# An attention and expert kernel: the first expert's weight splits, its row gather and the loop's tail put in another order

## The chip, the cores and the metric

One core of a Trainium2 chip runs the whole program in one launch. The metric is the device time of the execution in microseconds (us), the median of several runs.

## The reference

Two steps follow each other. Attention: 8 batches, 8 heads, 576 positions, 64 channels; heads 0 to 3 look at a local band of 32 positions, heads 4 to 7 at every 32nd position:

```python
scores = np.where(masks, q @ k.transpose / sqrt(D), -1e9)
x = softmax(scores) @ v                # then 4608 tokens of 512 channels
```

Then a mixture of 8 experts with one expert a token. A token with `x @ w_skip <= 0` is passed through; any other goes to the expert with the largest logit:

```python
e = argmax(x @ w_gate);  gate = softmax(x @ w_gate)[e]
out = x + gate * (relu(x @ w1[e]) @ w2[e])   # w1: 512 x 1024, w2: 1024 x 512
```

## The kernel before, in words

**The attention loop.** The main loop runs over 32 iterations (b, pr): 8 batches and in each four units of blocks, pr 0 and 1 of the local heads, pr 2 and 3 of the strided ones. An iteration issues the score products of the unit two ahead (`qk`, L200), the value products of the unit before (`pv`, L273 and L287), transposes and exponentials of its own (`tex`, L243 on PE, L251 on ACT) and the transposes of the finished output of two units before (`xpose`, L331 and L341). DVE adds the mask (`sm`, L207 to L214), finds the maxima (`mx`, L220) and scales the output (`x`, L300); POOL subtracts the maxima (L223).

**Routing.** When a group of batches is through, `score` multiplies its tokens with the gate (L387), `route1` transposes the scores (L406) and finds expert and gate on DVE (`rm`, L414, and the steps behind it), with the gate sums on POOL (L434 to L438). `route2` ranks the tokens (L447 to L454) and gives each its slot (`rdi`, L463); `scat` then writes tile after tile into a table in DRAM, by indirect transfers of POOL (L476).

**The first expert.** After batch 3 the expert with the most tokens so far is picked. For it, 288 of its tokens of batches 0 to 5 are taken early: `rows` reads their table rows (`tab`, L621), `gather` fetches the tokens from DRAM (`xg`, three indirect transfers of 96 rows, L633), and `xturn` transposes them on PE (L655). Its weights come in eight pieces of 512 KB, j 0 to 3 of w1 and 4 to 7 of w2: `wdma` fetches one into one of three buffers `raw` (L581, SP), `wcast` casts it on ACT (`w1h`, L593), and `wrest` takes the rest on DVE (`w1l`, L598). The products then take three matmuls for one: high by high, high by low, low by high. While the loop runs, all four pieces of w1 and the first of w2 are fetched, and the four are split.

**Behind the loop.** `ffn1a` computes the first two groups of hidden channels (L700, L704, with `hout` at L673 and L674), then `ffn1` the other six, with the last batch's routing in between; then come the second product and seven more experts.

**What sets the order.** Within the loop POOL, PE, DVE and SP keep the order in which the code is written (a manual schedule, L847); ACT is not among them there, its order is laid out by the scheduler. Behind the loop PE, ACT and DVE are in written order. Each engine works its own queue in order and waits at an instruction whose input isn't there.

Of the kernel before, what the change touches and what calls it, by code (L numbers as in the profile page):

```python
# [39 lines left out]
COUNTED = {4: 3, 7: 5}  # L40
PB = 3
CB = 5
SPLITS = [(6, 0), (6, 1), (7, 0), (7, 2)]
FETCH = [(6, 0), (6, 1), (6, 3), (7, 0)]
CE = (96, 3)
WHOLE = range(6)

# [52 lines left out]
def attn_moe(ctx: ExitStack, tc: tile.TileContext, q, k, vl, vh, vs, w9d, w1d, w2d, cst, out, NB=B):  # L100
    nc = tc.nc
    V, A, G, T = nc.vector, nc.scalar, nc.gpsimd, nc.tensor
# [413 lines left out]
    def count(b):  # L516
        n, _ = cnt_[b]
        t2 = constp.tile([1, NE], F32, name="pt2")
        V.tensor_tensor(t2, first, n, op=ALU.mult)
        r2 = constp.tile([1, 1], F32, name="pr2")  # L520
        V.tensor_reduce(r2, t2, axis=AX.X, op=ALU.add)
        V.scalar_tensor_tensor(fsel[:, 2:3], r2, float(CE[0] * CE[1]), fsel[:, 1:2], op0=ALU.min, op1=ALU.add)
        V.tensor_copy(isel[:, 2:3], fsel[:, 2:3])
# [64 lines left out]
    def wcast(key, j):  # L588
        raw = raw_.pop((key, j))
        pl, tg, nb = (early, "w1", 4) if j < 4 else (pool["h"], "w2", 2) if j < 6 else (pool["b"], "w2", 4)  # L590
        hi = pl.tile([128, 1024], F32R, name=tg + "h", tag=tg + "h", bufs=nb)
        lo = pl.tile([128, 1024], F32R, name=tg + "l", tag=tg + "l", bufs=nb)
        A.copy(hi, raw)  # L593
        cast_[key, j] = raw, hi, lo

    def wrest(key, j):
        raw, hi, lo = cast_.pop((key, j))
        V.tensor_tensor(lo, raw, hi.bitcast(F32), op=ALU.subtract)  # L598
        wt[key, j] = (hi, lo)

    def wsplit(key, j0, j1):
        for j in range(j0, j1):
            wcast(key, j)
            wrest(key, j)
# [214 lines left out]
    def run(*gs):  # L819
        weave(gs, [])  # L820
# [32 lines left out]
    for n, (b, pr) in enumerate(units):  # L853

        if n == 4:
            tv = table.rearrange("(p a n) c -> p a (n c)", p=128, a=5)
            fills = [(tv[:, a], fill.rearrange("p n c -> p (n c)")) for a in range(5)]
        if pr % 2 == 0:
            vj = jobs_v(b + 1, pr // 2) if b + 1 < NB else []
            g = n // 2 + 3  # L860
            qk_ = jobs_qk(g // 2, g % 2) if g // 2 < NB else [None] * 4
            ob = jobs_out(units[n - 4][0], units[n - 4][1] // 2) if n > 3 else [[], []]
            steps = [vj[0:1], vj[1:], ob[0], qk_[0:1], qk_[1:2], qk_[2:3], qk_[3:4], ob[1]]
            steps = [[x for x in y if x is not None] for y in steps]
        if n + LA >= len(units) and "h" not in pool:
            zctx.close()
            pool["h"] = ctx.enter_context(tc.tile_pool(name="hpool", bufs=1, side="right", reuse_waits="tile"))
        g = [i for i, x in enumerate(GROUPS) if x[1] == b]

        front = [qk(*units[n + LA])] if n + LA < len(units) else []  # L870
        if n > 0:
            front.append(pv(*units[n - 1]))
        seq = [tex(b, pr)]
        if g and pr == 2:
            seq = [xpose(*units[n - 2])] + seq
        for x in front[:-1]:
            next(x)
        hand()

        if len(front) > 1:  # L880
            run(seq.pop(0))
        hand()
        next(front[-1])
        hand()
        issue(fills[0:1], mark[0].ins)
        del fills[0:1]
        rank = []
        if ranked is not None:
            rank = [route2(ranked, of=COUNTED.get(b - 1))]
            for _ in range(tiles(ranked) + 1):  # L890
                next(rank[0])
            ranked = None

        if b > CB:
            run(*late)
            late = []
        for x in front:
            next(x, 0)
        run(*rank, *late, *front)
        late = []  # L900
        if cast_:
            wrest(*list(cast_)[0])
        if b > 0 and pr == 2:
            seq = [score(b - 1)] + [rest_out(b - 1)] * (b - 1 in WHOLE) + seq
        if n > 1 and not (g and pr == 2):
            seq.append(xpose(*units[n - 2]))
        run(*seq)
        hand()
        if pr == 3:
            issue(rest_, mark[0].ins)  # L910
            del rest_[:]
        if g and pr == 2:
            late = [route1(g[0])]
            next(late[0])
        if g and pr == 3:
            if b > CB:
                run(route2(g[0], of=COUNTED.get(b)))
            else:
                ranked = g[0]
        if b == PB + 2 and pr == 2:  # L920
            pick(PB)
        if (b, pr) in SPLITS:
            j = SPLITS.index((b, pr))
            wcast("e", j)
        if b == CB + 2 and pr == 3:
            count(CB)
        if n == 0 or pr == 3 and b + 1 < NB:
            for m in range(2):
                shift(b + (n > 0), m)
        if n == 1:  # L930
            for g in range(len(GROUPS)):
                payload(g)
        for _ in range(3 if b > CB else 2):
            if sc_ and n + 1 < len(units):
                scat(*sc_.pop(0))
        if b == PB + 2 and pr == 3:
            e0 = nc.sync.value_load(isel[0:1, 0:1], min_val=0, max_val=NE - 1)
            wdma("e", e0, 0, 1)
        if b == PB + 2 and pr == 3:
            s0 = G.value_load(isel[0:1, 1:2], min_val=0, max_val=(NE - 1) * ESTR)  # L940
        if (b, pr) in FETCH:
            j = FETCH.index((b, pr)) + 1
            wdma("e", e0, j, j + 1)
        if b == CB + 2:
            if pr == 0:
                assert not sc_
            if pr == 1:
                rows("e", s0, *CE, eng=G)
                gather("e", "e", "e", last=(CB + 1) * S)
    pool_order.close()  # L950
    nr = len(GROUPS) - 1
    while sc_:
        scat(*sc_.pop(0))
    with tc.manual_schedule(engines={T.engine, A.engine, V.engine}):
        run(pv(*units[-1]), xpose(*units[-2]), xturn("e"), xpose(*units[-1]))
    for kind in range(2):
        for part in jobs_out(NB - 1, kind):
            issue(part)
# [3 lines left out]
    psum, bufs = pctx.enter_context(tc.tile_pool(name="psumT", bufs=1, space=PSUM, reuse_waits="tile")), {"S": 2, "T": 3, "PV": 2, "R": 1}  # L962
    ga = ffn1a("e")
    with tc.manual_schedule(engines={T.engine, A.engine, V.engine}):
        run(ga, score(NB - 1))
        g = ffn1("e", 2, 6)
        run(islice(g, 4), later(route1, nr), islice(g, 4), later(route2, nr))
        while sc_:
            scat(*sc_.pop(0))
        wsplit("e", 4, 5)  # L970
        places = sort(NB - 1)
        run(g)
        rest = places()
        actx.close()
        pool["b"] = ctx.enter_context(tc.tile_pool(name="bpool", bufs=1, reuse_waits="tile"))
        wsplit("e", 5, 6)
        run(ffn1("e", 6, 8))
# [155 lines left out]
```

## Time and profile before

| | us |
|---|---|
| runs: median (lowest to highest of 3) | 447.95 (439.43 to 449.22) |
| the profiled execution, its own time | 444.14 |
| its span, first to last instruction | 442.4 |
| PE busy | 410.5 (93%) |
| DVE, ACT, POOL busy | 256.6, 197.7, 163.0 |

The attention loop ends near 167 us, the experts fill the rest. A row of a timeline names its start, its duration, engine, line, output and inputs, and in brackets the idle time of the engine just before it with what ended it. A busy PE is not PE at its peak: the granted clock (PEclk) stands beside it, 1.00 for 2.4 GHz and 0.50 for 1.2 GHz.

### The profile page before, as it was taken

How to read it: one execution, taken by the hardware profiler on the slowest of the kernel's cores; microseconds unless marked ns; L12 is line 12 of the kernel's file. 1: busy time of each engine (PE TensorE's matmuls, PEld its weight loads, DVE VectorE, ACT ScalarE, POOL GpSimd, SP SyncE). 2: the span in 40 equal slices, each digit the busy share in tenths (PEclk: the TensorE clock that was granted, in tenths of full speed). 3: DMA queues.
4: the chain of work that ended last, by engine and by line, in shares of the span. 5: the costliest groups of instructions: out<-in, count | busy, mean ns of one | idle time of the engine just before them, and what ended most of it. 6: DMA issues, size and time to landing. Idle time of an engine off the chain costs nothing.

```text
span 442.4 us, 12541 instructions
## 1 busy us (share of the span) xinstructions
PE 410.5 (93%) x5111; PEld 373.4 (84%) x5112; DVE 256.6 (58%) x500; ACT 197.7 (45%) x382; POOL 163.0 (37%) x205
## 2 busy tenths in 40 slices
PE   5999998999976984999999999999999999999994
PEld 3878787787765774899898799999999999999984
DVE  3686767659854964352494654474574554855611
ACT  1566373745626543342633434353543544554400
POOL 3353427745783667254043235022024122200201
PEclk8799999999988897999999999999999999999999
DMA  8999899999998536443557377365575565645201
GB/s 278 363 315 304 266 315 264 265 293 284 218 265 273 135 81 170 110 97 90 192 176 237 102 220 241 100 203 158 180 218 177 172 211 177 216 156 163 70 21 43
DMA packets 48758, 86.47 MB, mean 195 GB/s; under 512 B 9811, under 2 KB 25939, under 8 KB 48697
## 3 DMA queue, kind: packets, MB, share of 16 engines
q1 hardware_dynamic: 41017, 75.22, 56.1%
q0 software_dynamic: 7680, 10.42, 8.4%
q8 instruction: 41, 0.67, 0.6%
q14 instruction: 20, 0.16, 0.1%
HBM read 70.58 MB, written 15.63 MB: 195 GB/s over the span
## 4 chain that ended last, share of the span: by engine, by line
PE 53%; DMA 4%; issue 2%; POOL 2%; DVE 0%; POOLq 0%; ACT 0%; ACTq 0%
PE S L661 15%; PE S L663 15%; PE S L662 15%; DMA xg<-out_dram,tab 2%; DMA table<-pay,rdi 2%; PE T L655 2%; PE PV L753 2%; POOL xg L633 1%; PE S L700 1%; PE PV L795 0%; POOL table L476 0%; DMA tab<-table 0%; PE PV L794 0%; PE PV L793 0%; PE T L387 0%
## 5 line engine op out<-in xcount | busy, mean ns | idle before, releaser
L741 POOL DMA_INDIRECT out_dram<-ot,tab x25 | 27.9, 1117 | 149.2 <-DVE ot L739 135.7
L661 PE MATMUL S<-xh,w1h 128*128 128x342 f32 (+6 forms) x248 | 78.5, 316 | 0.3 <-DVE hl L674 0.3
L663 PE MATMUL S<-xh,w1l 128*128 128x342 f32 (+6 forms) x248 | 76.7, 309 | 0.0
L662 PE MATMUL S<-xl,w1h 128*128 128x342 f32 (+6 forms) x248 | 76.6, 309 | 0.0
L661 PE MATMUL S<-hh,w2h 128*128 128x288 f32 (+5 forms) x192 | 59.3, 309 | 0.0
L663 PE MATMUL S<-hh,w2l 128*128 128x288 f32 (+5 forms) x192 | 58.1, 303 | 0.0
L662 PE MATMUL S<-hl,w2h 128*128 128x288 f32 (+5 forms) x192 | 57.9, 302 | 0.0
L673 ACT ACTIVATE hh<-S 128x342 fp32r<-128x342 f32 (+6 forms) x64 | 28.0, 437 | 65.9 <-PE S L663 58.7
L598 DVE TENSOR_TENSOR w1l<-raw,w1h 128x1024 fp32r<-128x1024 f32 x32 | 39.3, 1232 | 27.0 <-ACT w1h L593 27.0
L661 PEld LDWEIGHTS S<-xh,w1h 128*128 128x128 f32 x248 | 46.9, 189 | 1.1 <-DVE hl L674 0.6
L598 DVE TENSOR_TENSOR w2l<-raw,w2h 128x1024 fp32r<-128x1024 f32 x32 | 39.0, 1223 | 13.7 <-ACT w2h L593 9.6
L200 PE MATMUL S<-kt,qt 64*64 64x54 f32 (+1 forms) x1280 | 33.6, 248 | 14.3 <-issue 4.3
L662 PEld LDWEIGHTS S<-xl,w1h 128*128 128x128 f32 x248 | 46.8, 189 | 0.1
L663 PEld LDWEIGHTS S<-xh,w1l 128*128 128x128 f32 x248 | 46.7, 188 | 0.0
L633 POOL DMA_INDIRECT xg<-out_dram,tab x25 | 32.5, 1302 | 35.3 <-PE T L655 13.9
L674 DVE SCALAR_TENSOR_TENSOR hl<-S,hh 128x342 fp32r<-128x342 f32 (+6 forms) x64 | 31.0, 484 | 24.0 <-ACT hh L673 23.8
L200 PEld LDWEIGHTS S<-kt,qt 64*64 64x64 f32 x1280 | 27.8, 145 | 19.8 <-DVE sm L207 6.8
L476 POOL DMA_INDIRECT table<-pay,rdi x38 | 39.7, 1044 | 10.8 <-issue 7.3
L223 POOL TENSOR_TENSOR sm<-sm,mx 128x384 f32<-128x384 f32 (+1 forms) x32 | 29.2, 935 | 35.8 <-DVE mx L220 29.3
L663 PEld LDWEIGHTS S<-hh,w2l 128*128 128x128 f32 x192 | 36.2, 189 | 0.1
L662 PEld LDWEIGHTS S<-hl,w2h 128*128 128x128 f32 x192 | 36.3, 189 | 0.0
L661 PEld LDWEIGHTS S<-hh,w2h 128*128 128x128 f32 x192 | 36.2, 188 | 0.0
(168 smaller groups left out, 828.3 us busy)
## 6 DMA issues: line engine op xcount, KB each, us to landing
raw<-in_w_dram SPq DMA_DIRECT2D x64, 512.0 KB
vt<-in_vs_dram SPq DMA_DIRECT2D x16, 390.0 KB
qt<-in_qp_dram SPq DMA_DIRECT2D x16, 304.0 KB
kt<-in_kp_dram SPq DMA_DIRECT2D x16, 297.0 KB
kt<-in_kp_dram SPq DMA_DIRECT2D x14, 304.0 KB
vt<-in_vl_dram SPq DMA_DIRECT2D x16, 260.0 KB
out_dram<-x SPq DMA_DIRECT2D x16, 256.0 KB
qt<-in_qp_dram SPq DMA_DIRECT2D x14, 288.0 KB
```

Source lines behind the costliest of these rows:

```text
L200: mark[0] = T.matmul(s[HP * (i ^ j):HP * (i ^ j) + HP, j, (blk - b0) * win:(blk - b0 + 1) * win], lhsT=qt[p, j, blk * nq:blk * nq + HP], r ...
L223: G.tensor_tensor(e[:, j], sw[:, j], mx[:, j].unsqueeze(2).broadcast_to([128, b1 - b0, win]), op=ALU.subtract)
L476: i = G.indirect_dma_start(out=table, out_offset=bass.IndirectOffsetOnAxis(ap=di[:, t:t + 1], axis=0), in_=pay[:, t, :], in_offset=None, b ...
L598: V.tensor_tensor(lo, raw, hi.bitcast(F32), op=ALU.subtract)
L633: i = G.indirect_dma_start(out=xg[:s["P"], t, :], out_offset=None, in_=out[0:last, :], in_offset=bass.IndirectOffsetOnAxis(ap=s["tab"][:s[ ...
L655: T.transpose(t[:, j * P:(j + 1) * P], s["xg"][:P, j, c * 128:(c + 1) * 128], ident[:P, :P])
L661: T.matmul(p, lhsT=a[0], rhs=b[0], start=start, stop=False)
L662: T.matmul(p, lhsT=a[0], rhs=b[1], start=False, stop=False)
L663: T.matmul(p, lhsT=a[1], rhs=b[0], start=False, stop=stop)
L673: A.activation(s["hh"][:, f, :C], p[:, :C], AF.Relu)
L674: V.scalar_tensor_tensor(s["hl"][:, f, :C], p[:, :C], 0.0, s["hh"][:, f, :C].bitcast(F32), op0=ALU.max, op1=ALU.subtract)
L741: i = G.indirect_dma_start(out=out, in_=ot[:P], in_offset=None, bounds_check=NTOK - 1, oob_is_err=False, out_offset=bass.IndirectOffsetOnA ...
```

## The change

Four things change. The splits of the first expert's pieces 0, 1 and 2 go from iterations (6,0) to (7,3) into (6,3) to (7,3): casts in (6,3), (7,0), (7,1), rests in (7,1), (7,2), (7,3); piece 3 is split behind `ffn1a`. The fetches follow: pieces 0 to 2 in (6,0), (6,1), (6,3), where pieces 1 to 3 were, and pieces 3 and 4 in (7,2) and (7,3). The scatters left over in (7,0) are issued ahead of that iteration's POOL work, and the gather of the first expert's tokens goes from (7,1) to (7,3), behind the gate sums of batch 6. At the loop's end `route2` of batch 6 stands behind the last `pv`, and the last `xpose` and the last batch's `score` stand ahead of `xturn`.

```diff
@@ -40,8 +40,9 @@
 COUNTED = {4: 3, 7: 5}
 PB = 3
 CB = 5
-SPLITS = [(6, 0), (6, 1), (7, 0), (7, 2)]
-FETCH = [(6, 0), (6, 1), (6, 3), (7, 0)]
+CASTS = [(6, 3), (7, 0), (7, 1)]
+RESTS = [(7, 1), (7, 2), (7, 3)]
+FETCH = [(6, 0), (6, 1), (6, 3), (7, 2), (7, 3)]
 CE = (96, 3)
 WHOLE = range(6)
 
@@ -896,10 +897,13 @@
             late = []
         for x in front:
             next(x, 0)
+        if b == CB + 2 and pr == 0:
+            while sc_:
+                scat(*sc_.pop(0))
         run(*rank, *late, *front)
         late = []
-        if cast_:
-            wrest(*list(cast_)[0])
+        if (b, pr) in RESTS:
+            wrest("e", RESTS.index((b, pr)))
         if b > 0 and pr == 2:
             seq = [score(b - 1)] + [rest_out(b - 1)] * (b - 1 in WHOLE) + seq
         if n > 1 and not (g and pr == 2):
@@ -913,17 +917,14 @@
             late = [route1(g[0])]
             next(late[0])
         if g and pr == 3:
-            if b > CB:
+            if b == CB + 1:
                 run(route2(g[0], of=COUNTED.get(b)))
             else:
                 ranked = g[0]
         if b == PB + 2 and pr == 2:
             pick(PB)
-        if (b, pr) in SPLITS:
-            j = SPLITS.index((b, pr))
-            wcast("e", j)
-        if b == CB + 2 and pr == 3:
-            count(CB)
+        if (b, pr) in CASTS:
+            wcast("e", CASTS.index((b, pr)))
         if n == 0 or pr == 3 and b + 1 < NB:
             for m in range(2):
                 shift(b + (n > 0), m)
@@ -935,24 +936,26 @@
                 scat(*sc_.pop(0))
         if b == PB + 2 and pr == 3:
             e0 = nc.sync.value_load(isel[0:1, 0:1], min_val=0, max_val=NE - 1)
-            wdma("e", e0, 0, 1)
         if b == PB + 2 and pr == 3:
             s0 = G.value_load(isel[0:1, 1:2], min_val=0, max_val=(NE - 1) * ESTR)
         if (b, pr) in FETCH:
-            j = FETCH.index((b, pr)) + 1
+            j = FETCH.index((b, pr))
             wdma("e", e0, j, j + 1)
         if b == CB + 2:
             if pr == 0:
                 assert not sc_
             if pr == 1:
                 rows("e", s0, *CE, eng=G)
+            if pr == 3:
                 gather("e", "e", "e", last=(CB + 1) * S)
     pool_order.close()
     nr = len(GROUPS) - 1
+    with tc.manual_schedule(engines={T.engine, A.engine, V.engine}):
+        run(pv(*units[-1]), xpose(*units[-2]), route2(ranked, of=CB))
+        count(CB)
+        run(xpose(*units[-1]), score(NB - 1), xturn("e"))
     while sc_:
         scat(*sc_.pop(0))
-    with tc.manual_schedule(engines={T.engine, A.engine, V.engine}):
-        run(pv(*units[-1]), xpose(*units[-2]), xturn("e"), xpose(*units[-1]))
     for kind in range(2):
         for part in jobs_out(NB - 1, kind):
             issue(part)
@@ -962,7 +965,8 @@
     psum, bufs = pctx.enter_context(tc.tile_pool(name="psumT", bufs=1, space=PSUM, reuse_waits="tile")), {"S": 2, "T": 3, "PV": 2, "R": 1}
     ga = ffn1a("e")
     with tc.manual_schedule(engines={T.engine, A.engine, V.engine}):
-        run(ga, score(NB - 1))
+        run(ga)
+        wsplit("e", 3, 4)
         g = ffn1("e", 2, 6)
         run(islice(g, 4), later(route1, nr), islice(g, 4), later(route2, nr))
         while sc_:
```

DVE, iterations (6,1) to (6,2), `mx<-sm_83` being the maxima of (6,3)'s unit. Before:

```order
L300 TENSOR_TENSOR x_2634<-PV,rc 128x2x128 x2
L220 TENSOR_REDUCE mx<-sm_83 128x10
L598 TENSOR_TENSOR w1l<-raw,w1h 128x1024
L207 TENSOR_TENSOR sm_80<-S,cs 128x768
L294 TENSOR_SCALAR rc<-PV 128x12
L295 RECIPROCAL rc<-rc 128x12
L300 TENSOR_TENSOR x_2634<-PV,rc 128x3x128 x2
L220 TENSOR_REDUCE mx<-sm_80 128x8
L598 TENSOR_TENSOR w1l<-raw,w1h 128x1024
L414 TENSOR_REDUCE rm<-T 128x5
```

And after the change:

```order
L301 TENSOR_TENSOR x_2629<-PV,rc 128x2x128 x2
L221 TENSOR_REDUCE mx<-sm_83 128x10
L208 TENSOR_TENSOR sm_80<-S,cs 128x768
L295 TENSOR_SCALAR rc<-PV 128x12
L296 RECIPROCAL rc<-rc 128x12
L301 TENSOR_TENSOR x_2629<-PV,rc 128x3x128 x2
L221 TENSOR_REDUCE mx<-sm_80 128x8
L415 TENSOR_REDUCE rm<-T 128x5
```

Both splits `w1l` have left this stretch.

POOL, iterations (7,0) to (7,3); `frame` is the subtraction for the strided heads, `rex`, `rz` and `rmk` are the gate sums. Before:

```order
L223 TENSOR_TENSOR sm_81<-sm_81,mx 128x480 x2
L476 DMA table<-pay_93,rdi 40960x4 x3
L223 TENSOR_TENSOR frame_84<-sm_82,mx 128x6x54 x2
L476 DMA table<-pay_93,rdi 40960x4 x2
L223 TENSOR_TENSOR frame_85<-sm_83,mx 128x5x54 x2
L621 ISA
L621 DMA tab<-table 96x12
L633 DMA xg<-out_dram,tab 96x512 x3
L434 TENSOR_TENSOR rex<-rex 128x5x4
L434 TENSOR_TENSOR rex<-rex 128x5x2
L435 TENSOR_TENSOR rz<-rex 128x5
L436 TENSOR_SCALAR rz<-rz 128x5
```

And after the change:

```order
L224 TENSOR_TENSOR sm_81<-sm_81,mx 128x480 x2
L477 DMA table<-pay_93,rdi 40960x4 x5
L224 TENSOR_TENSOR frame_84<-sm_82,mx 128x6x54 x2
L224 TENSOR_TENSOR frame_85<-sm_83,mx 128x5x54 x2
L622 ISA
L622 DMA tab<-table 96x12
L435 TENSOR_TENSOR rex<-rex 128x5x4
L435 TENSOR_TENSOR rex<-rex 128x5x2
L436 TENSOR_TENSOR rz<-rex 128x5
L437 TENSOR_SCALAR rz<-rz 128x5
L439 TENSOR_SCALAR rmk<-rmw 128x5
L634 DMA xg<-out_dram,tab 96x512 x3
```

The five scatters stand in one row ahead of both subtractions, and the gather stands behind the gate sums.

PE, the end of the loop, from the last matmul of `route2`. Before:

```order
L489 LDWEIGHTS oneb
L489 MATMUL T<-run_69,oneb 128x8
L287 MATMUL PV<-vt_2688,pts 64x65 x20
L341 MATMUL T<-cs,x_3186 128x128 x6
L655 MATMUL T<-cs,xg 128x96 x12
L341 MATMUL T<-cs,x_3186 128x128 x5
L700 MATMUL S<-xh,w1h 128x288
```

And after the change:

```order
L490 LDWEIGHTS oneb
L490 MATMUL T<-run_69,oneb 128x8
L342 MATMUL T<-cs,x_3170 128x128 x5
L388 MATMUL T<-xT_3144,w_65 32x144 x8
L388 MATMUL T<-xT_3288,w_65 32x144 x8
L656 MATMUL T<-cs,xg 128x96 x12
L701 MATMUL S<-xh,w1h 128x288
```

The last value products (`PV<-vt`) and the first part of the last transposes now lie ahead of `route2`; the last five transposes and the router products (`T<-xT`) lie ahead of the transposes of the gathered rows (`T<-cs,xg`).

## Rows read from the trace of the kernel before

**Rows 1.** The page's part 2: PE's busy tenths in 40 slices.
```profile
PE   5999998999976984999999999999999999999994
```

**Rows 2.** Windows: busy us of each engine, granted clock, DMA share, GB/s.
```profile
140.00:150.00 10.00, 8.64 (x177) 7.18 (x181) 9.62 (x22) 5.65 (x11) 3.54 (x7) 0.66 0.42 122
...
170.00:175.00 5.00, 2.31 (x13) 1.97 (x13) 2.20 (x12) 1.17 (x3) 3.52 (x7) 0.62 0.53 138
175.00:180.00 5.00, 5.00 (x30) 4.98 (x28) 0.98 (x4) 1.38 (x5) 2.43 (x3) 0.70 0.66 104
```

**Rows 3.** PE's timeline, first wait: start, us, line, idle before and its releaser.
```profile
136.95 0.47 PE L406 MATMUL T<-cs,s9s 9*128 9x9 f32 x5
141.36 1.88 PE L200 MATMUL S<-kt,qt 64*64 64x96 f32 x40 [3.94 <-DVE sm L207]
```

**Rows 4.** DVE's timeline, same stretch.
```profile
131.55 0.70 DVE L220 TENSOR_REDUCE mx<-sm 128x10 f32<-128x540 f32 x1
139.22 1.23 DVE L598 TENSOR_TENSOR w1l<-raw,w1h 128x1024 fp32r<-128x1024 f32 x1 [6.96 <-ACT w1h L593]
...
143.48 1.22 DVE L598 TENSOR_TENSOR w1l<-raw,w1h 128x1024 fp32r<-128x1024 f32 x1
144.61 0.20 DVE L414 TENSOR_REDUCE rm<-T 128x5 f32<-128x40 f32 x1
```

**Rows 5.** ACT's timeline, same stretch.
```profile
135.26 0.59 ACT L334 COPY xT<-T 128x512 f32<-128x512 f32 x1 [3.57 <-PE T L387]
...
138.16 1.03 ACT L593 CAST w1h<-raw 128x1024 fp32r<-128x1024 f32 x1
...
141.37 1.04 ACT L593 CAST w1h<-raw 128x1024 fp32r<-128x1024 f32 x1
```

**Rows 6.** PE's timeline, second wait.
```profile
169.82 0.27 PE L655 MATMUL T<-cs,xg 96*128 96x96 f32 x1 [3.11 <-DMA xg<-out_dram,tab]
172.65 2.43 PE L655 MATMUL T<-cs,xg 96*128 96x96 f32 x11 [2.55 <-DMA xg<-out_dram,tab]
174.87 1.27 PE L341 MATMUL T<-cs,x 128*128 128x128 f32 x5
...
180.14 1.66 PE L387 MATMUL T<-xT,w 128*32 128x144 f32 x32
```

**Rows 7.** POOL's timeline: subtractions, scatters, table read, third gather.
```profile
115.56 1.64 POOL L223 TENSOR_TENSOR sm<-sm,mx 128x384 f32<-128x384 f32 x2
...
143.72 2.44 POOL L223 TENSOR_TENSOR sm<-sm,mx 128x384 f32<-128x384 f32 x2 [6.38 <-DVE mx L220]
...
157.68 1.79 POOL L476 DMA_INDIRECT table<-pay,rdi  x1 [0.17 <-issue]
159.77 0.98 POOL L476 DMA_INDIRECT table<-pay,rdi  x1 [0.30 <-issue]
...
163.37 0.61 POOL L621 DMA_DIRECT2D tab<-table  x1 [1.36 <-issue]
...
168.74 0.96 POOL L633 DMA_INDIRECT xg<-out_dram,tab  x1 [0.30 <-issue]
```

**Rows 8.** The chain of waits: the third gather's transfer.
```profile
168.74 4.42 DMA xg<-out_dram,tab
```

**Rows 9.** DVE's timeline, end of the loop and first hidden groups.
```profile
161.69 0.20 DVE L414 TENSOR_REDUCE rm<-T 128x5 f32<-128x40 f32 x1 [1.69 <-PE T L406]
...
171.24 0.17 DVE L463 TENSOR_TENSOR rdi<-rds,rmk 128x5 int32<-128x5 f32 x1 [3.18 <-POOL rmk L438]
...
180.17 0.98 DVE L674 SCALAR_TENSOR_TENSOR hl<-S,hh 128x288 fp32r<-128x288 f32 x2 [4.17 <-ACT hh L673]
```

**Rows 10.** SP's queue: the second and third weight fetch handed over.
```profile
127.58 1.52 SPq L581 DMA_DIRECT2D raw<-in_w_dram  x1
...
132.74 0.83 SPq L581 DMA_DIRECT2D raw<-in_w_dram  x1
```

**Rows 11.** PE's timeline, a wait without a releaser.
```profile
126.17 0.34 PE L200 MATMUL S<-kt,qt 64*64 64x54 f32 x9 [2.16 <-issue]
```

## The prediction

> **What bounds the kernel now.** I read the page's forty slices first. PE stands at nine tenths or more nearly all along; what there is to win lies in slices 10 to 16, where it falls to 4 [rows 1]. In the expert part behind it PE is the bound, so a microsecond gained before the first expert's second weight group is a microsecond at the end. Then I took the windows, and the timelines of PE, DVE, ACT and POOL over the loop's last two batches. Two waits stand out.
>
> The first is at 137.4 to 141.4. PE idles 3.94 us, waiting for `sm` (L207) of DVE [rows 3]. DVE stood 6.96 us in front of the first `w1l`, waiting for its cast on ACT [rows 4]. ACT had that cast behind the copies and exponentials of iteration (6,2), which themselves waited for PE's router products (L387) [rows 5]. So PE waits for DVE, DVE for ACT, ACT for PE; it is an order, not a slow transfer. POOL had been idle 6.38 us for the same reason [rows 7]. DVE is then packed, 9.62 of 10 us in 140 to 150, while PE's clock is mixed (0.66) [rows 2]: in that stretch DVE sets the pace.
>
> The second is at 166.7 to 172.65. PE waits for the first expert's rows `xg`, 3.11 and then 2.55 us [rows 6]; the third gather is handed over at 168.74 and takes 4.42 us [rows 7, 8]. Behind it PE's granted clock is 0.62 and 0.70 on the mean [rows 2]: with the levels 2.4 and 1.2 GHz that is 3.8 + 3.0 us at the lower one, some 5.4 of them busy, which costs 2.7.
>
> **The change, part by part.**
>
> *Splits out of batch 6.* The first two `w1l` leave (6,1) and (6,2). DVE is free at 131.55 + 0.70 = 132.25 [rows 4]. The steps between the two old splits (sm, rc, x, mx) took 143.48 - 140.45 = 3.0 us, so DVE is through them by about 135.3 to 136.5. It then waits for the router transposes (L406), which end at 136.95 + 0.47 = 137.42 [rows 3], and starts `rm` at about 137.45 instead of 144.61 [rows 4]. From there DVE runs as before. **Gain 7.16 us**, and PE's lower clock behind the wait goes with it at no further price, as DVE paces that stretch. What is late next: the pv results and POOL's subtractions, both free by then (POOL idles from 137.3 [rows 7]).
>
> *The same splits later.* Piece 0 takes piece 2's old slot in (7,1): nothing. Piece 1 comes in (7,2) right before `rm`, where DVE idled 1.69 us [rows 9]; a split is 1.22: covered. Piece 2 stands in (7,3) between the two halves of the last x. Piece 3 goes behind the first two hidden groups; DVE was busy 0.98 and ACT 1.38 of 5 us there [rows 2], so 1.22 and 1.04 are covered, and its weights are due only at the seventh group. The casts: ACT had two of them (2.1 us) in the shadow of the first wait; now they stand between the exponentials of (7,0), where ACT has room, barely. Taken as nothing, bound 2.1 (below nothing: no reason).
>
> *Five scatters in a row, gather behind the gate sums.* POOL's work before the table read is the same: five scatters, two subtractions. The read (163.37) had 1.36 us of idle before it [rows 7], which bounds a gain. On the other side, a split on DVE slows POOL: the subtraction pair beside a `w1l` took 2.44 instead of 1.64, a scatter 1.79 instead of 0.98 [rows 4, 7]: 0.8 each. The new `w1l` in (7,2) falls on a subtraction, the one in (7,3) on the gather. The Trainium skill ("SBUF — State Buffer", Who interferes with whom) has this as a rule: a VectorE instruction with two SBUF inputs and a GpSimd one that reads SBUF exclude each other, and the later fully blocks. By that rule a hit could cost a whole split, 1.2 us, and the upper bound of the gather below would be 4.4 instead of 3.6; the trace shows 0.8 twice, so it agrees that one blocks the other, in part. The gate sums took POOL from the third gather's hand-over (168.74 + 0.96) to `rdi` at 171.24, 1.5 us [rows 7, 9]; they now run while the table row is under way, so they cost the gather nothing, and `rdi` no longer waits 3.18 us for them [rows 9].
>
> *Weight fetches.* The fetches of pieces 3 and 4 move to (7,2) and (7,3) on SP; each needs a buffer that a rest of the iteration before gives back. Piece 6 now waits for piece 3's split behind `ffn1a`, and on SP only the fetch of piece 7 and the other experts' tables stand behind it: nothing. Piece 4's 0.52 MB meets the gather; at the 260 GB/s that 138 GB/s at a share of 0.53 make at full share [rows 2] it is 2.0 us. The gather's landing is thus bounded between 1.36 earlier and 0.8 + 0.8 + 2.0 = 3.6 later. I take **0.5 later**: POOL's slack and one hit cancel about, and the engines had nearly half their time free there.
>
> *Transposes and router products ahead of the rows.* Without the wait in `rdi` the last x is ready near 169, so the last transposes (1.27 at the lower clock) and L387 (1.66) [rows 6] run inside the wait that stood until 172.65. Behind it, L387 is saved whole, 1.66; of the transposes half, 0.63, since at the lower clock something else takes their place. But L387 also covered the hand-back of the first S tile: `hl` of the first group ends at 180.17 + 0.49 = 180.66 [rows 9], L387 began at 180.14: the third group now stands 0.52. Together **1.66 + 0.63 - 0.52 - 0.50 = 1.27 us**. `route2` and the count move ten small DVE instructions behind the last x, and five scatters behind the gather: hidden, since nothing waits for them before the other experts' tables are read. The lower clock I keep as long as before (bound: 2.7 won, nothing lost).
>
> **Sum.** 444.14 - 7.16 - 1.27 = 435.7, rounded up to **436.0 us**. The profiled execution is 3.8 under the median of the three runs and 4.7 over the lowest; its own time is near the middle of the four, so I leave the sum there (on the median's footing it would be 439.8, on the lowest run's 431.3).
>
> **Rivals.**
> 1. *The second wait closes.* The gather lands 1.36 early instead of 0.5 late, and PE's busy time before it keeps the clock: 1.9 + 2.7 more, 431.3. For: PE has 2.6 us of new work inside the wait. Against: it still has none from 166.7 (169.82 - 3.11 [rows 6]) to about 169, and up to 2 us behind L387; a single wait of 2.16 us at 124 to 126.2 [rows 11] is not much less. That wait has no releaser in the trace; it can be longer or shorter with any other order of the fetches, one more reason for the margins below. Chance 0.15.
> 2. *The gather comes late.* Both hits on POOL and the whole of piece 4's transfer: 3.6 instead of 0.5, 439.1. For: the hits are there in the order; the fetch is handed over ahead of the last stores. The Trainium skill's page "DMA: Bandwidth & Descriptors" (Queues, rings and completion order) says that an engine takes turns between the queues it has work for; by that a gather shares with the fetch and does not wait behind it, which would halve the 2.0. No row here shows it. Chance 0.20.
> 3. *ACT takes the place of the first wait.* Casts and the `v` copies (4.2 us of ACT in the old wait's shadow [rows 5]: 138.16 to 142.41) now compete with the exponentials; if all of it showed, 440.2. Against: ACT idles 3.57 us at once before L334 [rows 5]. Chance 0.10.
> 4. *Slower: a cast that waits for its fetch.* ACT is in order, and the second cast stands ahead of the copies that give back PE's transpose tiles. Its fetch now leaves at about 132.7 and the cast comes up near 145, 12 us later; before, the fetch handed over at 127.58 was cast at 141.37, 13.8 us later, with no idle time of ACT [rows 5, 10]. From a landing later than 12 us each microsecond goes to ACT, then PE; beyond 20 us the whole gain is gone, at 22 the time is 446. Nothing in the trace took so long. Chance 0.04.
>
> My forecast has 0.51.
>
> **Range and chances.** The unknowns of the sum give 431 to 439 by rivals 1 and 2, the spread of the runs some 4 more to each side; with 2 in 10 left out, 430.0 to 443.0. Two per cent (9 us) is about what a measurement of this kernel can tell from no change; against the median of 447.95 faster means under 439.0. The forecast is there about 8 times in 10, rival 1 always, rival 2 four in ten, rival 3 hardly: 0.41 + 0.15 + 0.08 + 0.01, and less where executions near the lowest of before are the measure: faster 0.60, within 0.36, slower 0.04.
>
> **What would show it.** Right: no idle time of DVE before a `w1l` in batch 6, no wait of PE near 137, `rm` of batch 6 about 7 us earlier; `xg`'s transposes behind L387, one wait of about 2 us before them. Wrong: PE or DVE waiting for a cast or a copy of ACT in (6,3) or (7,0) (rivals 3, 4); a gather that takes over 6 us from hand-over (rival 2); or a full clock from 165 on (rival 1). If the first wait turns out to be a late transfer that merely moves, the main term falls and the time stays near 443.

## The result, and the profile after

| | kernel before | changed kernel |
|---|---|---|
| median of 20 runs each (lowest to highest), us | 445.05 (439.43 to 449.22) | 439.35 (435.44 to 441.63) |
| the profiled execution: its own time, span, us | 444.14, 442.4 | 440.55, 438.9 |
| ratio, 95% interval | | 0.9896 [0.9864, 0.9929] |

The forecast was 436.0, in 430.0 to 443.0. The kernel got faster by 1.0%, less than the two per cent from which the forecast counts a kernel as faster: 5.7 us by the medians and 4.6 by the ratio, where the forecast had 8.1. The page's slices of the changed kernel, to be held against [rows 1]:

```profile
PE   5989999899979876999999999999999999999994
```

The 6 of the first wait has become a 9, the 4 of the second a 6. The profile after runs 1.71 us late before the change tells (ACT's `xT` in (6,2) at 136.97, before 135.26 [rows 5]; the same copy in (5,2), where nothing was changed, is already 1.77 late, 114.97 for 113.20). I take that off where I compare positions, and call it "net". PE's timeline, in the columns of [rows 3] and [rows 6]:

```profile
139.06 1.06 PE L201 MATMUL S<-kt,qt 64*64 64x96 f32 x40
...
147.01 0.33 PE L288 MATMUL PV<-vt,pts 54*64 54x65 f32 x4 [1.21 <-issue]
...
164.99 1.67 PE L388 MATMUL T<-xT,w 128*32 128x144 f32 x32
166.59 0.30 PE L656 MATMUL T<-cs,xg 96*128 96x96 f32 x1
168.65 0.30 PE L656 MATMUL T<-cs,xg 96*128 96x96 f32 x1 [1.76 <-DMA xg<-out_dram,tab]
170.80 1.86 PE L656 MATMUL T<-cs,xg 96*128 96x96 f32 x10 [1.85 <-DMA xg<-out_dram,tab]
177.78 0.40 PE L662 MATMUL S<-xh,w1h 128*128 128x288 f32 x1 [0.47 <-DVE hl L675]
```

The score products at 139.06 wait for nothing; the 3.94 of [rows 3] are gone. The router products stand inside the second wait, of which 3.61 are left. The third hidden group at 177.78 is the place where the gain is handed to the expert part; in the kernel before it stood at

```profile
181.74 0.40 PE L661 MATMUL S<-xh,w1h 128*128 128x288 f32 x1
```

so it comes 3.96 earlier, net 5.67. DVE's timeline of the changed kernel, against [rows 4] and [rows 9]:

```profile
139.17 0.20 DVE L415 TENSOR_REDUCE rm<-T 128x5 f32<-128x40 f32 x1 [1.03 <-PE T L407]
139.71 1.07 DVE L421 SCALAR_TENSOR_TENSOR req<-rd,cs 128x40 f32<-128x40 f32 x1
...
157.53 0.20 DVE L415 TENSOR_REDUCE rm<-T 128x5 f32<-128x40 f32 x1 [0.39 <-PE T L407]
```

`rm` in (6,2), the one that the prediction calls `rm` of batch 6, comes 5.44 earlier, net 7.15. `rm` in (7,2) comes 4.16 earlier (161.69 in [rows 9]), net 5.87: 1.28 went on the way. POOL's timeline, against [rows 7], and SP's queue:

```profile
139.08 1.64 POOL L224 TENSOR_TENSOR sm<-sm,mx 128x384 f32<-128x384 f32 x2
...
153.86 3.79 POOL L224 TENSOR_TENSOR frame<-sm,mx 128x324 f32<-128x324 f32 x4
157.60 0.59 POOL L622 DMA_DIRECT2D tab<-table  x1
...
163.63 1.23 POOL L634 DMA_INDIRECT xg<-out_dram,tab  x1 [0.30 <-issue]
```

```profile
162.17 0.76 SPq L582 DMA_DIRECT2D raw<-in_w_dram  x1
```

And the chain of waits, against [rows 8]:

```profile
163.63 7.13 DMA xg<-out_dram,tab
```

The third gather is handed over net 6.82 earlier and lands net 4.11 earlier: its transfer takes 7.13 and not 4.42 us. Between the first hand-over (160.96) and the second (162.35) SP gave out piece 4's fetch. The windows, against [rows 2]:

```profile
165.00:170.00 5.00, 2.19 (x35) 1.26 (x34) 0.92 (x8) 1.74 (x6) 3.59 (x4) 0.89 0.94 304
170.00:175.00 5.00, 4.20 (x21) 4.20 (x22) 1.83 (x4) 1.60 (x4) 1.33 (x2) 0.50 0.62 163
175.00:180.00 5.00, 4.53 (x33) 4.12 (x32) 2.14 (x3) 2.10 (x4) 0.00 (x0) 0.92 0.11 43
```

While the gather is under way the DMA engines are busy (0.94; before, 0.73 and then 0.53 in the two windows of its gather, 165 to 175). Behind the second wait PE's granted clock is again at the lower level, 1.2 GHz (0.50), for all of 170 to 175.

### The profile page after: what moved, and what is told of

Its sections match the earlier page's. It is cut to its first block, busy times and chain, and to the rows that moved or that the text cites. A ratio compares the mean times of both kernels' runs of the same rounds, so it can differ in the third digit from the quotient of the medians.

```text
span 438.9 us, 12546 instructions
## 1 busy us (share of the span) xinstructions
PE 409.8 (93%) x5111; PEld 372.1 (85%) x5112; DVE 258.2 (59%) x500; ACT 197.5 (45%) x382; POOL 162.9 (37%) x205
## 4 chain that ended last, share of the span: by engine, by line
PE 75%; DMA 10%; issue 5%; DVE 5%; POOL 2%; ACT 2%; SPq 1%; POOLq 0%; DVEq 0%; ACTq 0%
PE S L662 15%; PE S L664 15%; PE S L663 15%; PE T L244 5%; PE S L201 5%; PE PV L274 4%; DMA out_dram<-x 3%; DMA xg<-out_dram,tab 3%; PE PV L288 2%; PE T L656 2%; PE T L342 2%; PE PV L754 2%; DMA table<-pay,rdi 2%; PE T L388 1%; PE T L332 1%
## 5 line engine op out<-in xcount | busy, mean ns | idle before, releaser
L477 POOL DMA_INDIRECT table<-pay,rdi x38 | 38.7, 1018 | 11.0 <-issue 8.0
L201 PE MATMUL S<-kt,qt 64*64 64x54 f32 (+1 forms) x1280 | 32.6, 244 | 7.7 <-issue 3.4
L201 PEld LDWEIGHTS S<-kt,qt 64*64 64x64 f32 x1280 | 26.8, 142 | 13.3 <-issue 5.4
L659 DVE TENSOR_TENSOR xl<-T,xh 128x288 fp32r<-128x288 f32 (+7 forms) x30 | 13.4, 469 | 39.8 <-ACT xh L658 39.7
```

Source lines behind the costliest of these rows:

```text
L201: mark[0] = T.matmul(s[HP * (i ^ j):HP * (i ^ j) + HP, j, (blk - b0) * win:(blk - b0 + 1) * win], lhsT=qt[p, j, blk * nq:blk * nq + HP], r ...
L477: i = G.indirect_dma_start(out=table, out_offset=bass.IndirectOffsetOnAxis(ap=di[:, t:t + 1], axis=0), in_=pay[:, t, :], in_offset=None, b ...
```

## The experiments

Experiments that were timed together ran on one chip, and the chips (0, 1 and 6, as the results number them; the one of the first runs has no number) are not alike: the kernel before took 443.28 us on chip 0, 452.76 on chip 1, 452.22 and 451.19 on chip 6. So every ratio is to the kernel before timed beside it.

| run | chip | median, us | ratio to before [95%] |
|---|---|---|---|
| e1 splits and fetches alone | 1 | 448.71 | 0.9906 [0.9871, 0.9941] |
| e2 scatters, gather and tail alone | 1 | 462.21 | 1.0207 [1.0164, 1.0250] |
| e3 piece 4 fetched behind the loop | 1 | 466.46 | 1.0298 [1.0257, 1.0339] |
| e4 gather ahead of the gate sums | 1 | 455.85 | 1.0051 [1.0021, 1.0082] |
| the changed kernel | 6 | 455.67 | 1.0063 [1.0026, 1.0100] |
| e5 ranking behind the hidden groups | 6 | 455.07 | 1.0082 [1.0048, 1.0116] |
| e6 scatters in two rows | 6 | 453.12 | 1.0023 [0.9988, 1.0058] |
| e7 e4, e5 and e6 together | 6 | 452.92 | 0.9990 [0.9956, 1.0023] |
| the kernel before, one run | 0 | 439.36 | |
| e8 e1, fetches 3 and 4 earlier | 0 | 439.87 | 0.9922 [0.9886, 0.9958] |
| e9 three scatters written later, one run | 0 | 435.37 | |
| e10 changed kernel, fetches 3 and 4 earlier | 6 | 455.19 | 1.0092 [1.0053, 1.0131] |

**e1: the splits and fetches alone.** On the kernel before:

```diff
-SPLITS = [(6, 0), (6, 1), (7, 0), (7, 2)]
-FETCH = [(6, 0), (6, 1), (6, 3), (7, 0)]
+CASTS = [(6, 3), (7, 0), (7, 1)]
+RESTS = [(7, 1), (7, 2), (7, 3)]
+FETCH = [(6, 0), (6, 1), (6, 3), (7, 2), (7, 3)]
...
         run(ga, score(NB - 1))
+        wsplit("e", 3, 4)
```

> The kernel before with the new places of the splits and fetches alone; scatters, gather and the loop's tail stay as before. Theory (the splits bring the gain, the tail nothing): rm of batch 6 starts near 139 as in the changed kernel (5.4 us before the 144.61 of the kernel before), and the time is 438.5 to 441.0, within 1.5 us of the changed kernel. Rival (the splits only fill another wait, the tail brings the gain): 443 to 446, within 2 us of the kernel before.

Measured: 448.71, 4.05 under the kernel before. The microseconds of the expectation were for the first chip; as a ratio it is what the whole change gave there. That the splits bring the gain is borne out by the time. `rm` of batch 6 starts at 144.14 and not near 139: no split and no wait for `sm` stand before it any more, but the whole trace runs later on this chip (ACT's `xT` at 139.82), and PE's router transposes wait 1.54 for `s9s`. Its chain of waits and SP's queue:

```profile
170.82 6.93 DMA xg<-out_dram,tab
```

```profile
170.98 0.27 SPq L582 DMA_DIRECT2D raw<-in_w_dram  x1
```

Here too piece 4's fetch is handed over right beside the third gather, and here too the gather takes 7 us.

**e2: the rest of the change alone.** The changed kernel with SPLITS, FETCH and the calls of `wcast` and `wrest` of the kernel before.

> The changed kernel with the splits and fetches where they were before; scatters, gather and tail as changed. Theory (the tail brings next to nothing where piece 4's fetch lies beside the gather; here that fetch is an iteration earlier): the third gather lands 4.4 to 5.0 us after its hand-over, the first wait of PE near 137 is there again with 3.5 to 4.2 us, and the time is 1 to 3 us under the kernel before, 442 to 444. Rival (the tail brings the gain): 4 to 6 us under it, 439 to 441.

Measured: 462.21, 9.45 slower than the kernel before; both theories fall. DVE's first `w1l`, PE, and ACT:

```profile
143.04 1.22 DVE L598 TENSOR_TENSOR w1l<-raw,w1h 128x1024 fp32r<-128x1024 f32 x1 [9.06 <-ACT w1h L593]
```

```profile
182.41 1.96 PE L387 MATMUL T<-xT,w 128*32 128x144 f32 x32
184.31 0.96 PE L655 MATMUL T<-cs,xg 96*128 96x96 f32 x9
190.92 0.74 PE L655 MATMUL T<-cs,xg 96*128 96x96 f32 x3 [5.65 <-ACT s9s L392]
```

```profile
189.71 1.16 ACT L392 COPY s9s<-T 9x144 f32<-9x144 f32 x4 [6.73 <-remote]
```

The first wait is back with the splits (PE stands 4.07 at L200). But the gathered rows are no longer waited for: nine of the twelve transposes run straight behind the router products. The last three need the tile of T that holds those products' result, and its copy `s9s` starts at 189.71, 5.3 us after the products' end (184.37). "Remote" means that the profile names no releaser. The 5.65 are a part of the 9.45; where the rest lies was not followed up.

**e3 and e4: the fetch behind the loop, the gather ahead of the gate sums.** On the changed kernel, e3 and then e4:

```diff
-FETCH = [(6, 0), (6, 1), (6, 3), (7, 2), (7, 3)]
+FETCH = [(6, 0), (6, 1), (6, 3), (7, 2)]
...
-    wdma("e", e0, 5, 7, st_["e"]["taken"])
+    wdma("e", e0, 4, 7, st_["e"]["taken"])
```

```diff
             if pr == 1:
                 rows("e", s0, *CE, eng=G)
-            if pr == 3:
                 gather("e", "e", "e", last=(CB + 1) * S)
```

> The changed kernel with piece 4's fetch handed over behind the loop, not in (7,3). Theory (the fetch beside the gather stretches its transfer from 4.4 to 7.1 us): the third gather lands 4.4 to 5.0 us after its hand-over, the transposes of the gathered rows start 2.0 to 2.7 us earlier, and the time is 1.5 to 2.7 us under the changed kernel, 436.5 to 438. Rival (the output stores stretch it): the gather takes 6.5 us or more, the time within 0.7 us of the changed kernel. Second rival (the fetch does, but its cast is then late): gather 4.4 to 5.0, an idle time before the cast of piece 4, no gain.

> The changed kernel with the gather handed over in (7,1) again, ahead of the gate sums of batch 6 on POOL. Theory (the gather's landing bounds the tail, the gate sums are not in the way of anything): the third gather is handed over about 1.5 us earlier, ahead of most of piece 4's fetch, and lands 1.5 to 3.5 us earlier; the time is 1 to 3 us under the changed kernel. Rival (the gate sums on POOL hold up rdi and with it the last x and the last transposes): rdi waits 1.5 to 3 us for POOL and the time is the same or up to 2 us over the changed kernel.

Measured: 466.46 and 455.85, DVE's timeline of e3:

```profile
206.64 1.23 DVE L599 TENSOR_TENSOR w2l<-raw,w2h 128x1024 fp32r<-128x1024 f32 x1 [5.04 <-DMA table<-pay,rdi]
```

In both, as in e2, PE waits for `s9s` (5.42 and 4.16) and not for the gather, so what the gather gained could not show. In e3 the second product starts 7.03 late as well, waiting for the last `hl`, which stand on DVE behind a split of w2 that itself waits 5.04, by the profile for the scatters. Piece 4's own split, though fetched 7 us later, is in time (198.07, in e4 197.43); why the order and the wait came out so is open. The late copy had to be understood first.

**The changed kernel again, and e5 to e7.** In e2 to e4 the copy starts when POOL has just handed over its last row of five scatters, those of the ranking at the loop's end. e5 takes that ranking, with its scatters, behind the first hidden groups; e6 leaves out the three lines that put five scatters in a row in (7,0); e7 has e4, e5 and e6.

```diff
-        run(pv(*units[-1]), xpose(*units[-2]), route2(ranked, of=CB))
-        count(CB)
+        run(pv(*units[-1]), xpose(*units[-2]))
         run(xpose(*units[-1]), score(NB - 1), xturn("e"))
-    while sc_:
-        scat(*sc_.pop(0))
...
-        run(ga)
+        run(ga, route2(ranked, of=CB))
+        count(CB)
+        while sc_:
+            scat(*sc_.pop(0))
```

> The changed kernel itself, once more, beside the variants that follow. Theory (the order of the tail is at fault in the variants with the late copy s9s): it behaves here as in its own run, 0.985 to 0.994 of the kernel before, and s9s (L393) of the last batch starts within 1.5 us of the router products' end. Rival (the place of the five scatters of POOL decides, whatever stands in the tail): the transposes of the gathered rows wait 4 to 6 us for s9s here too, and the ratio is 1.00 to 1.02.

> The changed kernel with the ranking of batch 6 (route2) and the count, and with them its five scatters on POOL, behind the first two hidden groups. Theory (a row of scatters on POOL holds up what PE reports as done, so that s9s comes up to 6 us late): no wait of s9s over 1.5 us, the time 2 to 6 us under the changed kernel beside it. Rival (s9s is late for another reason, the scatters only stand beside it): the wait of 4 us or more stays, and the time is within 1 us of the changed kernel.

> The changed kernel with the scatters of (6,3) and (7,0) in two rows of three and two, around a subtraction, as in the kernel before. Theory (the row of five holds up PE): PE's waits without a releaser in the value products of (7,0) shrink from about 2 to 3 us in all to under 1.5, and the time is 1 to 4 us under the changed kernel. Rival (the row does no harm, it brings the table read forward): the table read is 1 to 2 us later and the time the same or up to 2 us longer.

> The changed kernel with the ranking behind the hidden groups, the scatters in two rows, and the gather handed over in (7,1) ahead of the gate sums. Theory (each of the three gives back its part): the third gather lands 3 to 4.5 us after its hand-over, no wait for s9s, and the time is 5 to 9 us under the changed kernel, 0.97 to 0.98 of the kernel before. Rival (one wait takes the other's place; PE's end of the loop is bounded by the last x): within 2 us of the better of the other two variants.

Measured: the changed kernel is slower than the kernel before on chip 6, 1.0063; its rival holds there. POOL, PE and ACT of that run:

```profile
178.91 1.01 POOL L477 DMA_INDIRECT table<-pay,rdi  x1 [4.36 <-DVE cnt L495]
```

```profile
178.86 2.15 PE L388 MATMUL T<-xT,w 128*32 128x144 f32 x32
...
187.33 0.74 PE L656 MATMUL T<-cs,xg 96*128 96x96 f32 x3 [5.05 <-ACT s9s L393]
```

```profile
186.12 1.15 ACT L393 COPY s9s<-T 9x144 f32<-9x144 f32 x4 [6.70 <-remote]
```

The rows of scatters are shown by their first; there are five, 1.27 to 1.32 us apart. This one lasts from 178.91 to 185.04, the copy starts at 186.12. In the first trace of the same kernel five scatters stood beside the same copy (165.50 to 171.63), and it started 0.12 us after the products (166.66), as ACT's timeline there shows:

```profile
166.78 1.16 ACT L393 COPY s9s<-T 9x144 f32<-9x144 f32 x4 [1.11 <-PE T L388]
```

In e5 the row is moved, to 190.95 to 197.36 (POOL, ACT, PE, DVE):

```profile
190.95 1.01 POOL L477 DMA_INDIRECT table<-pay,rdi  x1 [13.82 <-DVE cnt L495]
```

```profile
183.69 1.15 ACT L393 COPY s9s<-T 9x144 f32<-9x144 f32 x4 [1.71 <-PE T L388]
...
198.11 0.71 ACT L674 ACTIVATE hh<-S 128x288 fp32r<-128x288 f32 x2 [3.14 <-PE S L664]
```

```profile
183.50 1.87 PE L656 MATMUL T<-cs,xg 96*128 96x96 f32 x12
...
201.61 0.40 PE L662 MATMUL S<-xh,w1h 128*128 128x288 f32 x1 [3.37 <-DVE hl L675]
```

```profile
198.90 0.17 DVE L464 TENSOR_TENSOR rdi<-rds,rmk 128x5 int32<-128x5 f32 x1 [3.27 <-POOL rmk L439]
```

`s9s` comes in time, all twelve transposes run in one go; and at the new place of the row PE stands 3.37. Most of that is plain order: DVE waits 3.27 for the gate sums (`rmk`), which POOL has in its queue behind the scatters, and `hl` stands behind that step. ACT gets PE's results late there too, by some 1.5 us: the older of the two groups was through at 196.65, ACT starts on it at 198.11, 0.75 after the row. The time stays (455.07 against 455.67): the copy is freed, another wait comes in its place, and moving the row does not pay.

e5 moves the ranking's few matmuls along with its scatters; e6 leaves all but the scatters in place. In (7,0) PE's transposes for the exponentials (`ptl`, L252) end at 154.51 in the changed kernel and 154.94 in e6. ACT starts on them 3.87 later there, when the row of five is nearly through (158.87), and 2.46 later here, when the first row of three is (156.67):

```profile
158.38 0.59 ACT L252 ACTIVATE ptl<-T 96x512 f32<-96x512 f32 x1 [5.03 <-remote]
```

```profile
157.40 1.35 ACT L252 ACTIVATE ptl<-T 96x512 f32<-96x512 f32 x3 [3.09 <-remote]
```

The five waits without a releaser of the value products there shrink from 3.04 us in all to four of 1.23 in all, as expected, and the median is 2.55 lower, though the intervals overlap; the last row of five is left where it was, and with it the wait for `s9s` (4.68). That a row of scatters on POOL holds up what ACT sees of PE's work, and PE with it, is thus borne out on chip 6 by moving the row and by shortening it, not by taking it away. e7 shows both changes at once (twelve transposes in one go, a wait of 3.41 at the later row) and ends level with the kernel before, 0.9990: better than the changed kernel on that chip, and not as good as e1 on chip 1.

**The kernel before, e8 and e9 on chip 0.** e8 is e1 with `FETCH = [(6, 0), (6, 1), (6, 3), (7, 1), (7, 2)]`; e9 is the changed kernel with `for _ in range(2)` for `while sc_` at the loop's end.

> The kernel before itself, for its trace beside the experiments. Theory (rows of scatters on POOL hold up PE's reports on the chips of the experiments, and the order before had other work in their shadow): PE's value products show waits without a releaser beside the scatters here too, the router products of the last batch stand behind the first hidden groups and no copy s9s is waited for; the third weight group (L661) starts 4 to 8 us earlier than the 193.33 of the changed kernel in the same surroundings. Rival (the experiments' chips are only slower in all places): the trace is that of the first run with a longer loop, and the third group stands 3 us or more behind 193.

> The splits and fetches of the change with the tail of before, and the fetches of pieces 3 and 4 one iteration earlier, in (7,1) and (7,2), so that piece 4 has landed before the gather. Theory (the fetch beside the gather stretches it): the third gather lands 4.0 to 5.0 us after its hand-over, against 6.93 with the splits alone, and the time is 1.5 to 3 us under theirs, a ratio of 0.983 to 0.988. Rival (the output stores stretch it, or the earlier fetch waits for its buffer and delays the stores behind it): 6 us or more, ratio 0.989 to 0.995.

> The changed kernel with two of the five scatters of batch 6 handed over at the loop's end, and the other three behind those of batch 7. Theory (PE's reports come when the row of scatters is through): s9s of the last batch starts within 1.7 us of the end of the second scatter, so it waits 1.0 to 3.0 us and not 6.7, and the transposes of the gathered rows wait under 1.5 us for it. Rival (the first scatter, or something at this place in ACT's program, is enough): s9s still waits 5 us or more.

Chip 0 is like the chip of the first runs: no copy came late on it. So the expectation of the kernel before cannot be judged: its 193.33 is from chip 6. e9 tells nothing of its theories either: as built, POOL's order is that of the changed kernel, with the five scatters in one row, and so it is one more run of the changed kernel: 435.37, beside 443.28 as the median of the kernel before beside it. e8 missed its time (0.9922, not 0.983 to 0.988; the rival's range was 0.989 to 0.995), and these three traces show where. The kernel before: ACT's `s9s` in (6,2) as the mark, the chain, and PE:

```profile
132.72 1.15 ACT L392 COPY s9s<-T 9x144 f32<-9x144 f32 x4
```

```profile
165.71 3.55 DMA xg<-out_dram,tab
```

```profile
166.57 0.39 PE L655 MATMUL T<-cs,xg 96*128 96x96 f32 x1 [2.90 <-DMA xg<-out_dram,tab]
168.79 2.37 PE L655 MATMUL T<-cs,xg 96*128 96x96 f32 x11 [1.82 <-DMA xg<-out_dram,tab]
...
177.22 0.40 PE L661 MATMUL S<-xh,w1h 128*128 128x288 f32 x1
```

e8, the same, and POOL between:

```profile
136.56 1.15 ACT L393 COPY s9s<-T 9x144 f32<-9x144 f32 x4
```

```profile
159.06 0.61 POOL L622 DMA_DIRECT2D tab<-table  x1 [3.30 <-issue]
162.22 1.03 POOL L634 DMA_INDIRECT xg<-out_dram,tab  x1 [2.55 <-DMA out_dram<-x]
```

```profile
164.84 4.88 DMA xg<-out_dram,tab
```

```profile
166.64 0.40 PE L656 MATMUL T<-cs,xg 96*128 96x96 f32 x1 [6.39 <-DMA xg<-out_dram,tab]
167.60 0.42 PE L656 MATMUL T<-cs,xg 96*128 96x96 f32 x1 [0.56 <-DMA xg<-out_dram,tab]
169.77 1.86 PE L656 MATMUL T<-cs,xg 96*128 96x96 f32 x10 [1.74 <-DMA xg<-out_dram,tab]
...
177.60 0.40 PE L662 MATMUL S<-xh,w1h 128*128 128x288 f32 x1
```

e9:

```profile
133.79 1.15 ACT L393 COPY s9s<-T 9x144 f32<-9x144 f32 x4
```

```profile
159.32 7.08 DMA xg<-out_dram,tab
```

```profile
172.73 0.40 PE L662 MATMUL S<-xh,w1h 128*128 128x288 f32 x1 [0.46 <-DVE hl L675]
```

Net of the mark (3.84 and 1.07), the third group comes 3.46 earlier in e8 and 5.56 in e9. In e8 the transfer is 4.88, in the range expected, with piece 4's fetch handed over 10 us ahead of it (154.70); but PE waits 8.69 for the gathered rows, in the kernel before 4.72. DVE is through (7,2) some 7.3 us earlier (`rm` at 155.23, in the kernel before 158.66), the table read and the gather are not: POOL stands 3.30 before the read and 2.55 before the first gather, in the kernel before 1.35 and 1.59. The 2.55 ends with an output store, as in e8's rival, which has the stores delayed, and both fetches are now handed over ahead of stores and beside the scatters and the read; that they are the reason was not shown (e1, with the later fetches, also stands 2.44 before its read). In e9, with the row of five and the gather behind the gate sums, POOL goes into the read without a wait. So in e8 the splits bring 7.2 to the end of the loop, and 4.0 of it comes back as a longer wait for the gathered rows.

**e10: the changed kernel with e8's fetches.**

> The changed kernel with the fetches of pieces 3 and 4 one iteration earlier, in (7,1) and (7,2); nothing else. Theory (piece 4's fetch beside the gather is what made the gather late): the third gather lands 3.5 to 5.0 us after its hand-over and not 7.1; on a chip where the copy s9s does not come late, the time is 2 to 5 us under the changed kernel, a ratio to the kernel before of 0.978 to 0.986; on one where it comes late, PE waits for s9s and not for the gather, and the ratio is 0.998 to 1.007 as with the changed kernel there. Rival (the stores stretch the gather too, or the fetch now delays the scatters' transfers and so the table read): the gather takes 6 us or more, or the table read comes 1.5 us later, and the ratio stays at 0.987 to 0.993.

It ran on chip 6: 1.0092, the last three transposes wait 4.83 for the copy, which starts at 187.28 behind a row of scatters that ends at 186.90, and the ratio is a little over the 0.998 to 1.007 that the theory gave for this case. What it would do on a chip like the first is open.

## Why the prediction was right, and where it was not

The time lay in the range, 3.35 above the forecast. The direction and the first mechanism were right. The number that came is near that of rival 2 (439.1): the rival was right that piece 4's fetch would make the gather late, not that two hits on POOL would (the hand-over is 0.34 late). That the two figures meet to 0.25 is in part luck, since the forecast starts from one execution (444.14) and the result is a median of 20, and the executions of a kernel lie some 6 to 10 us apart.

- **Splits out of batch 6**, 7.16 at `rm`: measured 7.15 net, with the wait at L200 gone. Right, and on chip 0 it is 7.16 in both traces (`rm` at 141.59 in the kernel before, 138.27 in e8 and 135.50 in e9, less the 3.84 and 1.07 of the mark). "From there DVE runs as before" was off by 1.28: `req` took 1.07, beside POOL's subtraction (139.08 to 140.72), where it took 0.36 at this place in the kernel before, and PE's L288 stood 1.21 without a releaser, of which some 0.6 reached DVE.
- **The gather's landing** is the step that failed. I bounded it at 3.6 later and took 0.5, against a gain of 7.16 passed on whole. Measured, it came 3.05 later than that (4.11 earlier and not 7.16): 2.71 by the transfer, 0.34 by the hand-over. Gathers with piece 4's fetch handed over beside them took 7.13, 6.93 and 7.08 (the changed kernel, e1, e9); those without, 4.42, 3.55 and 4.88 (the kernel before twice, e8). The split on DVE that falls on the third hand-over in the changed kernel (1.23 us of POOL for 0.96) is not the reason: in e1 none falls on it (0.96), and the transfer takes 6.93 all the same. The reason given for 0.5, that the engines had nearly half their time free, did not hold: beside its stores and the fetch the share was 0.94, and the transfers beside the fetch are 2.2 to 3.5 longer (on chip 0, 7.08 against 4.88 and 3.55), more than the 2.0 estimated from its bytes. The Trainium skill ("DMA: Bandwidth & Descriptors", Queues, rings and completion order) says that an engine takes turns between the queues that it has work for; rival 2 concluded that this would halve the 2.0, and the traces do not bear that out.
- **The splits later, the casts**: ACT ran the casts in (6,3) and (7,0) without standing before them, so rivals 3 and 4 did not come (the one of (7,0) is at 146.34, also without a wait):

```profile
144.42 1.06 ACT L594 CAST w1h<-raw 128x1024 fp32r<-128x1024 f32 x1
```

  POOL's subtractions lost 1.12 beside the splits of (7,1) and (7,2), somewhat over the 0.8 that a hit was put at: four of them took 3.79, where 1.42 and 1.25 stood for the same four in the kernel before. POOL's slack covered it: the table read came net 7.48 earlier.
- **The tail**, without the gather 1.66 + 0.63 - 0.52 = 1.77: from the third gather's landing to the third hidden group it was 181.74 - 173.16 = 8.58 and is 177.78 - 170.76 = 7.02, so 1.56. Right in the first trace. But the five scatters behind the gather, put at nothing since nothing waits for them, were not hidden on chips 1 and 6: there `s9s` comes late beside them, PE waits 4.2 to 5.7 us for it (e2 to e4, e6, e10, the changed kernel), and the tail costs. e1 against the changed kernel is 0.9906 to 1.0063, some 7 us, on two chips that are alike in the kernel before.
- **The lower clock as long as before**: the means 0.89, 0.50 and 0.92 over 165 to 180 give 1.1 + 5.0 + 0.8 = 6.9 us at 1.2 GHz, before 6.8. Right; rival 1 did not come.

So 4.11 of the landing and 1.56 behind it make the 5.67 at the third group (5.3 at the end, 444.14 - 440.55 + 1.71). The sum had 8.43; of the 2.76 between them, 2.55 is the gather's landing (3.05 where 0.50 stood), 0.21 the tail. The 1.28 that DVE and PE lost on the way lies inside the wait for the gather and cost nothing further.

What stays open is why chips 1 and 6 hold up PE's reports beside scatters and chip 0 does not. The kernel before has no trace from those chips, so what the rows cost it there, and how much of its 8 to 9 us more there is that, was not seen; nor can it be excluded that taking the profile has a part in it.

## What to carry to other kernels

When a wait is removed, follow the gain to the next thing that is fetched: a gather's time of landing has its own chain (scatter, table read, hand-over, transfer), and it moves only as far as that chain does. In these traces a half-megabyte fetch handed over within 1.5 us of a small gather that is waited for goes with 2.2 to 3.5 us more for the gather. Putting the fetch an iteration earlier gave the gather its short transfer back (4.88, e8) and still did not bring the time expected: the gather was handed over net 2.75 us later than in e9 (161.00 against 158.25). So look at the whole chain before moving one piece of it. A rearrangement that brings 1% on one chip can lose as much on another: time it on more than one before keeping it; of the variants here, the splits without the new tail were under the kernel before on both chips they ran on, each with its own places for the last two fetches (0.9906, 0.9922).

## What was not expected of the hardware

- On chips 1 and 6, while POOL hands over scatters in a row (about 1.3 us each), PE's value products come in groups with waits of 0.2 to 1.1 us without a releaser, and ACT starts on finished results of PE up to 5.3 us after PE's end (`s9s`, 0.4 to 1.2 us after the end of the row in six traces). On chip 0, and in the first trace, the same row let the copy start 0.12 us after PE.
- A DVE instruction of 0.20 us on 40 columns (`req`) took 1.07 beside POOL's subtraction, and 0.36 beside one in the kernel before. The Trainium skill ("SBUF — State Buffer", Who interferes with whom) says that a VectorE instruction with two inputs in SBUF and a GpSimd one that reads SBUF contend; the trace agrees, in both directions (`req` up to 0.87 longer, POOL's four subtractions 1.12 longer beside the two splits).
